# A top-k attention and two MLPs: first granules in halves, a second transposed tile, shared PSUM banks

## The chip, the cores and the metric

The kernel runs on one core of one Trainium2 chip. The metric is the device time of one execution in microseconds. The kernel before takes 1304.58 us, the median of 3 runs (1304.22 to 1305.43).

## What is computed

```
scores = q @ k.T / 8                      # 4 batches, 8 heads, 576 tokens, 64 wide
keep the 32 largest of each row, the rest to -1e9
attn = softmax(scores); o = attn @ v
x = o as 2304 tokens x 512
h = x @ w_in;  y = (h * sigmoid(1.702 h)) @ w_out            # layer 1: 512 -> 2048 -> 512
h = y @ w_in2; g = P(h) / (Q(h) + 1e-6); out = g @ w_out2    # layer 2, P and Q polynomials
```

q, k, v are float32 and the four weight matrices come as float64. Most products are made of float16 high and low parts, three matmuls in place of one; the last product of layer 2 is in float32.

## The kernel before, in words

**Tiles.** The 2304 tokens are 18 tiles of 128. A head of a tile is the unit of attention: 18 x 8 = 144 heads, done in this order. `attend` makes the scores (L584, into one of two PSUM tiles S of two banks), takes the top 32 with four MAX8 (L593) and three match-replace (L595) on VectorE, which write a copy W, then Prelu into E (L598, ScalarE), a bias on GpSimd (L599, L600), the exponential (L601), a float16 copy A and its low part (L603, L605), and a DMA transpose from A into AT (L609). W and E have two tiles each, A two, AT one. `attend_av` multiplies AT with V into the PSUM tile misc (L624), takes a reciprocal on VectorE (L634) and scales into x on ScalarE (L635).

**Granules.** When a tile's 8 heads are done, `x_done` splits x and transposes it by DMA into xh (L690). Granules are groups of tiles for the MLPs: eight of two tiles and two of one (GRAN). A layer of a granule runs in units: `u_h` multiplies into the PSUM tile h (L747), `u_act` evicts and computes the gate on ScalarE, VectorE and GpSimd (L768 to L808), `u_o` multiplies into acc0 and acc1, one bank for each tile of the granule (L829 for layer 2, L832 for layer 1). A unit of a pair of tiles takes 256 hidden columns, a unit of one tile 512. `y_done` (L847 and on) copies acc away, scales and transposes y for layer 2, `o_done` (L883) writes the result out.

**PSUM** has 8 banks: S takes four, acc0 and acc1 one each, h one and misc one. misc also serves the small sums over partitions in `total` (L308).

**Weights.** `w_load` brings in 32 blocks of float64 words, 1 MB each (L346), and three VectorE operations (L353, L355, L357) make float32 of them in one of three work slots. Layer 1's blocks are scaled and split into W1, which stays in SBUF. Layer 2's are written back to DRAM (L364, L385) and come in again through a ring of 7 slots by `u_load` (L720) for each granule. The ring's memory is also that of the two load slots and the three work slots, so its first 7 loads wait for every split.

**Order.** No queue is ordered at run time. A planner in the kernel takes each operation with an estimated duration and a due time counted in heads, adds an offset for its kind, engine and phase (OFF, PHASES), and picks on each engine, among those that can start earliest, the one that is due first; that is the instruction order written out. The u_h operations are chained in program order. The due time of layer 1 of a granule is 4.59 heads behind its last tile (LAV + MLAG). SPLIT lists the granules whose layer 1 runs as two halves of one tile, and LAGS says how many granules layer 2 runs behind:

```
seq, g2 = [], 0
for g in range(NG):
    seq += first_layer(g)
    while g2 < NG and g >= min(g2 + LAGS[g2], NG - 1):
        seq.append((2, g2, None))
        g2 += 1
```

With SPLIT = (0, 7, 8) and LAGS of 1 the order of layer 1 (a) and layer 2 (b) is a0 in two halves, a1, b0, a2, b1, a3, b2 and so on; a7 is in halves, and a9, b8, b9 come last. Since u_h is chained, b0 can't start ahead of a1.

## Time and profile before

| | |
|---|---|
| median of 3 runs | 1304.58 us (1304.22 to 1305.43) |
| span of the profiled execution, first to last instruction | 1298.1 us |
| its own device time | not listed; the span lies 6.5 us under the median |
| TensorE / VectorE / ScalarE / GpSimd busy | 1054.5 / 1038.0 / 1046.1 / 967.9 us |
| mean granted TensorE clock | 0.953 |

Times in the profile count from the first instruction. PE is TensorE, PEld its weight loads, DVE VectorE, ACT ScalarE, POOL GpSimd, SP the engine that issues the DMAs. A busy share is the time in which at least one instruction ran on the engine. The granted clock is TensorE's, as a share of full speed.

### The profile page before, as it was taken

What the parts mean: (1) busy time and instruction counts of PE and PEld (TensorE: products, weight loads), DVE (VectorE), ACT (ScalarE), POOL (GpSimd) and SP (SyncE); (2) the same over time, 40 slices, a digit from 0 to 9 for tenths busy, and PEclk for the clock granted to TensorE, in tenths of its full rate; (3) what the DMA queues carried; (4) which work ended last, traced back from release to release, by engine and by line L of the source; (5) the groups of instructions that cost most, each with busy time, mean ns of one, the idle gap of its engine ahead of it and who ended that gap; (6) DMA issues with size and microseconds to landing.
All of it is one profiled execution on the core that took longest, in us unless ns stands there. A gap on an engine that the chain in (4) does not pass through costs nothing.

```text
span 1298.1 us, 25266 instructions
## 1 busy us (share of the span) xinstructions
PE 1054.5 (81%) x8812; PEld 709.2 (55%) x8812; DVE 1038.0 (80%) x2227; ACT 1046.1 (81%) x1930; POOL 967.9 (75%) x1243
## 2 busy tenths in 40 slices
...
GB/s 237 203 186 175 150 263 255 228 252 175 145 73 158 195 170 106 144 231 168 141 216 211 85 171 218 147 115 181 182 106 154 205 117 83 209 99 154 115 247 183
DMA packets 366144, 222.40 MB, mean 171 GB/s; under 512 B 316608, under 2 KB 328896, under 8 KB 366016
## 3 DMA queue, kind: packets, MB, share of 16 engines
...
## 4 chain that ended last, share of the span: by engine, by line
PE 33%; DVE 22%; ACT 16%; POOL 15%; DMA 7%; issue 6%; SPq 1%; POOLq 0%; DVEq 0%; ACTq 0%
PE h L747 14%; PE acc L829 7%; DVE mx L593 7%; PE acc L832 6%; DVE W L595 6%; ACT t L768 6%; DMA AT<-A 6%; POOL t L772 5%; POOL A L605 3%; DVE ring L357 3%; PE misc L624 2%; PE S L584 2%; DVE ring L355 2%; POOL nm L599 2%; ACT E L601 2%
## 5 line engine op out<-in xcount | busy, mean ns | idle before, releaser
L772 POOL TENSOR_TENSOR t<-t,t 128x512 f32<-128x512 f32 x288 | 375.8, 1306 | 134.7 <-ACT t L768 67.4
L593 DVE MAX8 mx<-W 128x8 f32<-128x576 f32 x432 | 324.7, 755 | 6.4
L829 PE MATMUL acc<-ring,t 128*128 128x512 f32 x576 | 269.6, 600 | 12.0 <-POOL t L772 11.0
L747 PE MATMUL h<-xh,W 128*128 128x128 f16 (+1 forms) x2304 | 211.8, 251 | 7.7 <-ACT t L768 6.8
L605 POOL TENSOR_TENSOR A<-E,A 128x576 f16<-128x576 f32 x143 | 189.7, 1327 | 34.5 <-ACT A L603 29.6
L595 DVE MATCH_REPLACE8 W<-mx,W 128x576 f32<-128x576 f32 x288 | 213.5, 741 | 0.0
L747 PE MATMUL h<-yh,ring 128*128 128x256 f16 (+1 forms) x1920 | 203.5, 263 | 6.1 <-ACT t L768 5.3
L747 PEld LDWEIGHTS <-W 128*128 128x128 f16 x2304 | 183.8, 101 | 33.1 <-issue 15.7
L747 PEld LDWEIGHTS <-ring 128*128 128x128 f16 x1920 | 171.8, 98 | 47.1 <-issue 27.8
L584 PE MATMUL S<-K,qs 128*128 128x288 f16 (+1 forms) x640 | 120.7, 320 | 84.3 <-ACT E L598 67.3
L832 PE MATMUL acc<-W,gh 128*128 128x512 f16 x576 | 175.2, 386 | 0.9 <-ACT gh L806 0.9
L829 PEld LDWEIGHTS acc<-ring,t 128*128 128x128 f32 x576 | 101.1, 190 | 102.4 <-issue 85.0
L624 PE MATMUL misc<-V,AT 128*128 128x65 f16 (+5 forms) x2400 | 107.2, 203 | 56.5 <-DMA AT<-A 48.8
L601 ACT ACTIVATE E<-E,nm,ei 128x576 f32<-128x576 f32 x144 | 125.1, 869 | 33.2 <-POOL nm L600 31.4
L624 PEld LDWEIGHTS <-AT 128*128 128x128 f16 (+2 forms) x2400 | 97.3, 106 | 97.9 <-DMA AT<-A 76.4
L776 DVE SCALAR_TENSOR_TENSOR t<-t,ab,t 128x512 f32<-128x512 f32 x72 | 61.2, 850 | 108.8 <-ACT t L768 108.5
L598 ACT ACTIVATE E<-S,mx 128x576 f32<-128x576 f32 x144 | 106.5, 739 | 42.2 <-DVE mx L593 39.2
L584 PEld LDWEIGHTS <-qs 128*128 128x128 f16 (+1 forms) x640 | 65.6, 110 | 129.6 <-issue 88.6
L768 ACT ACTIVATE t<-h,cf 128x512 f32<-128x512 f32 (+1 forms) x160 | 93.7, 642 | 47.1 <-PE h L747 32.8
L593 DVE MAX8 mx<-S 128x8 f32<-128x576 f32 x144 | 108.8, 757 | 27.2 <-PE S L584 22.0
L599 POOL TENSOR_SCALAR nm<-mx,ei 128x1 f32<-128x1 f32 x144 | 82.2, 571 | 44.9 <-DVE mx L593 35.7
L832 PE MATMUL acc<-W,gl 128*128 128x512 f16 x288 | 110.9, 385 | 5.4 <-POOL gl L808 5.3
...
## 6 DMA issues: line engine op xcount, KB each, us to landing
ring<-scr SPq DMA_DIRECT2D x160, 512.0 KB, 4.0
...
scr<-ring SPq DMA_DIRECT2D x8, 512.0 KB, 7.5
```

Of the source, the lines that this page charges most:

```text
L584: PE.matmul(s[:n, c, :SH], qs[:, 2 * (h % 4) + x, :n], K[:, h % 2, c * SH:(c + 1) * SH], start=(x == 0), stop=(x == 1))
L593: op("DVE", dve(S, not r), lambda r=r: DVE.max(mx[:, r], w.t if r else sv()), [w if r else s], [mx], prio)
L595: op("DVE", dve(S, not r) + 0.068, lambda r=r: DVE.match_replace(w.t if r else two(w.t), mx[:, r], w.t if r else sv(), NEG), [mx, w if r e ...
L599: op("POOL", 2 * PTINY, lambda: (POOL.tensor_scalar(nm.t, mx[:, 0, 0:1], mx[:, 3, 7:8], es(), ALU.subtract, ALU.mult), POOL.tensor_scalar( ...
L601: op("ACT", act(S) + 2 * APA, lambda: ACT.activation(e.t, e.t, AF.Exp, bias=nm.t, scale=es()), [e, nm, ei], [e], prio)
L605: lo = lambda en: en.tensor_tensor(A[:, 1, :S], e.t, A[:, 0, :S], ALU.subtract)
L624: PE.matmul(ps[r0:r0 + n, :hi - lo], at[:kp, x, j, r0:r0 + n], V[:kp, h % 2, j, lo:hi], start=(j == 0 and lo == D and x == 0), stop=(j == ...
L747: PE.matmul(o, w[:, half, kd * 256 + jj * P: kd * 256 + (jj + 1) * P], xy[:, tl, l * ND + kd, :], start=(n == 0), stop=(n == 3 * ND - 1))
L768: op("ACT", act(w, True) + APA, lambda f2=f2, c=c: ACT.activation(dst[:, c], src[:, c], func, bias=bias(f2) if bias else 0.0, scale=sc(f2) ...
L772: op("POOL", pool_tt(512), lambda: POOL.tensor_tensor(o.t, x.t, y.t, f), [x, y], [o], prio, alt=("DVE", dve(512), lambda: DVE.tensor_tenso ...
L829: PE.matmul(acc[j].t, u.gate[:, c], w[:, jj * DM:(jj + 1) * DM], start=st, stop=sp)
L832: PE.matmul(acc[j].t, l[:, c], w[:, half, jj * DM:(jj + 1) * DM], start=(st and n == 0), stop=(sp and n == 2))
```

## The change

What it does:

- **SPLIT** goes from (0, 7, 8) to (0, 1, 2, 7, 8), and **LAGS** begins with 0.5, 0.5. A layer 2 may now stand behind half a granule. The order becomes a0 in halves, first half of a1, b0, second half of a1, first half of a2, b1, second half of a2, a3, b2, a4 and so on as before.
- **Staged splits** (STAGE = 8): the first 8 of layer 1's 16 blocks are made float32 in the room of W1 that blocks 8 to 15 fill later, and only the later ones in the work slots. The first write to such room (the Square, L370) waits for the block staged there.
- **AT** has two tiles (NAT = 2).
- **W and E** become one buffer with three tiles (NE = 3).
- **h and misc** share two banks with the tag hm, and acc0 and acc1 become two banks of one tag acc. The planner hands these banks out in the order of use.
- **y_copy**: the copies of acc leave `y_done` and run for each tile as soon as its part of layer 1 ends. xh gets two fixed tiles.
- **The planner**: several estimated durations, the phases and nearly all offsets are new (some 250 offsets in place of 69), so the order on each engine changes. W2P, the due time of layer 2's weight blocks, goes from 4.62 to 3.4.

No instruction of the computation is added or removed, but for the shapes of halves in layer 1 of granules 1 and 2.

```diff
-            cv = slot("work", work)
+            n_w = 2 * f2 + j
+            over = []
+            if layer == 1:
+                region = lambda i: W1t[:, i // 2, 2 * (i % 2):2 * (i % 2) + 2].rearrange("p a n -> p (a n)")
+                if n_w < STAGE:
+                    cv = staged[2 * NPAIR - STAGE + n_w] = token(f"stage{n_w}")
+                    cv.t = region(2 * NPAIR - STAGE + n_w)
+                if n_w in staged:
+                    over = [staged.pop(n_w)] if n_w >= STAGE else []
+            if layer == 2 or n_w >= STAGE:
+                cv = slot("work", work)
...
             op("ACT", act(CW) + 0.2, lambda hl=hl, val=val, wi=wi: ACT.activation(
-                hl().rearrange("p a n -> p (a n)").bitcast(F32), val(), AF.Square, accum_out=wsq[:, f2, wi:wi + 1]), [cv], [dst, sqb], prio)
+                hl().rearrange("p a n -> p (a n)").bitcast(F32), val(), AF.Square, accum_out=wsq[:, f2, wi:wi + 1]), [cv], [dst, sqb] + over, prio)
...
     def misc():
-        return buf("misc", [P, 512], F32, NMISC, pp)
+        return buf("hm" if HM else "misc", [P, 512], F32, HM or NMISC, pp)
...
-        w = buf("W", [P, S], F32, 2)
-        e = buf("E", [P, S], F32, NE)
+        w = e = buf("W", [P, S], F32, NE)
...
-        u.ph = buf("h", [P, 512], F32, NH, pp)
+        u.ph = buf("hm" if HM else "h", [P, 512], F32, HM or NH, pp)
...
-                ACC[u.layer, u.g, j] = buf(f"acc{j}", [P, 512], F32, NACC, pp)
+                ACC[u.layer, u.g, j] = buf("acc", [P, 512], F32, NACC, pp)
...
+    def y_copy(g, tiles, prio):
+        for j in tiles:
+            aj = ACC.pop((1, g, j))
+            yc = YC[g, j] = buf("yc", [P, DM], F32, NYC)
+            op("ACT", act(512, True), lambda yc=yc, aj=aj: ACT.activation(yc.t, aj.t, AF.Copy), [aj], [yc], prio - 1e-3,
+               alt=("DVE", dve(512, True), lambda yc=yc, aj=aj: DVE.tensor_copy(yc.t, aj.t)))
...
-        seq += first_layer(g)
-        while g2 < NG and g >= min(g2 + LAGS[g2], NG - 1):
-            seq.append((2, g2, None))
-            g2 += 1
+        for n, part in enumerate(first_layer(g)):
+            seq.append(part)
+            while g2 < NG and g + (n + 1) / len(first_layer(g)) >= min(g2 + 1 + LAGS[g2], NG):
+                seq.append((2, g2, None))
+                g2 += 1
...
-NACC = 1
+NACC = 2
-NE = 2
+NE = 3
-NAT = 1
+NAT = 2
+NMISC = 1
+HM = 2
-SPLIT = (0, 7, 8)
-LAGS = (1, 1, 1, 1, 1, 1, 1, 1, 1, 1, 1, 1, 1, 1, 1, 1, 1, 1)
+SPLIT = (0, 1, 2, 7, 8)
+LAGS = (0.5, 0.5, 1, 1, 1, 1, 1, 1, 1, 1, 1, 1, 1, 1, 1, 1, 1, 1, 1, 1)
-W2P = 4.62
+W2P = 3.4
+STAGE = 8
...
-    ('attend', 'PE'): 0.16,
-    ('attend', 'PE', 0): 0.86,
+    ('attend', 'PE'): -11.3,
+    ('attend', 'PE', 0): 1.59,
+    ('attend', 'PE', 1): 4.16,
+    ('attend', 'PE', 2): 6.98,
+    ('attend', 'PE', 3): 4.46,
-    ('attend_av', 'PE', 0): 1.95,
+    ('attend_av', 'PE'): -5.57,
...
-PHASES = (16.0, 48.0, 130.0)
-FREE = ("t", "misc")
+PHASES = (1, 41.34, 154.07)
+FREE = ("t", "misc", "acc", "hm")
```

## Rows read from the trace of the kernel before

**Rows 1.** The page: busy totals of the engines.

```profile
PE 1054.5 (81%) x8812; PEld 709.2 (55%) x8812; DVE 1038.0 (80%) x2227; ACT 1046.1 (81%) x1930; POOL 967.9 (75%) x1243
```

**Rows 2.** By stretch: length; PE, PEld, DVE, ACT, POOL busy; clock; DMA share; GB/s.

```profile
0.00:300.00 300.00, 119.99 (x1034) 83.14 (x1035) 275.83 (x582) 205.94 (x370) 209.65 (x267) 0.88 0.83 218
300.00:345.00 45.00, 24.39 (x195) 15.43 (x193) 43.38 (x120) 32.45 (x76) 29.36 (x67) 0.54 0.79 152
345.00:600.00 255.00, 240.52 (x1996) 162.11 (x1996) 222.52 (x488) 228.11 (x425) 204.91 (x282) 0.99 0.69 154
600.00:1105.00 505.00, 487.95 (x4182) 330.38 (x4180) 466.28 (x988) 453.19 (x831) 412.43 (x533) 1.00 0.71 156
1105.00:1298.00 193.00, 181.68 (x1411) 118.18 (x1409) 29.98 (x54) 126.42 (x233) 111.53 (x98) 1.00 0.52 167
```

**Rows 3.** The same for instructions on ring alone (on DVE, the weight splits).

```profile
0.00:300.00 300.00, 0.00 (x0) 0.00 (x0) 117.76 (x96) 81.88 (x96) 54.35 (x24) 0.88 0.83 218
```

**Rows 4.** The same for mx alone: DVE, ACT, POOL; last the whole span.

```profile
0.00:300.00 300.00, 147.59 (x286) 20.55 (x28) 26.79 (x28) 0.88 0.83 218
300.00:345.00 45.00, 39.46 (x75) 5.09 (x7) 2.90 (x7) 0.54 0.79 152
...
sum 1298.00, DVE 774.03 ACT 106.45 POOL 82.17; mean DVE 258.01 ACT 35.48 POOL 27.39
```

**Rows 5.** Timeline of SP's queue: last split store, transposes of tiles 2, 3, 4, 5, 7.

```profile
276.19 0.34 SPq L385 DMA_DIRECT2D scr<-yh  x1
...
296.71 1.25 SPq L690 DMA_TRANSPOSE xh<-xs  x1
...
340.72 1.39 SPq L690 DMA_TRANSPOSE xh<-xs  x1
...
406.51 1.34 SPq L690 DMA_TRANSPOSE xh<-xs  x1
...
455.88 1.23 SPq L690 DMA_TRANSPOSE xh<-xs  x1
...
563.03 1.23 SPq L690 DMA_TRANSPOSE xh<-xs  x1
```

**Rows 6.** Timeline of PE: the first h of a layer of a granule.

```profile
345.02 2.74 PE L747 MATMUL h<-xh,W 128*128 128x256 f16 x12
...
401.79 1.47 PE L747 MATMUL h<-yh,ring 128*128 128x256 f16 x12
...
469.89 1.47 PE L747 MATMUL h<-xh,W 128*128 128x256 f16 x12
...
520.76 1.47 PE L747 MATMUL h<-yh,ring 128*128 128x256 f16 x12
...
580.51 2.78 PE L747 MATMUL h<-xh,W 128*128 128x256 f16 x24 [0.16 <-ACT t L768]
```

**Rows 7.** VectorE's waits, 345 to 600 us: us in total, times, longest.

```profile
DVE r L634 <- PE misc L624: 12.2, 9, 3.3
```

**Rows 8.** Timeline of VectorE: the first weight split.

```profile
14.45 1.34 DVE L353 TENSOR_SCALAR ring<-ring 128x1024 int32<-128x1024 int32 x1 [2.14 <-DMA ring<-in_moe_w_in_dram]
```

**Rows 9.** TensorE's waits, 345 to 1105 us.

```profile
PE misc L624 <- DMA AT<-A: 16.5, 18, 2.2
...
PE h L747 <- ACT t L768: 4.9, 7, 1.7
```

**Rows 10.** Timelines of VectorE and GpSimd: a head's first match-replace, its low part, a later head.

```profile
502.29 0.75 DVE L595 MATCH_REPLACE8 W<-mx,S 128x576 f32<-128x576 f32 x1
...
510.72 1.28 POOL L605 TENSOR_TENSOR A<-E,A 128x576 f16<-128x576 f32 x1 [0.31 <-ACT A L603]
...
521.91 0.75 DVE L595 MATCH_REPLACE8 W<-mx,S 128x576 f32<-128x576 f32 x1
```

**Rows 11.** The chain that ended last, in order of time: start, us, instructions.

```profile
508.60 2.62 PE h L747 x24
...
1074.36 2.68 PE h L747 x48
```

More of the change, by code (lines that the diff above doesn't have):

```diff
@@ L191, in schedule @@
             if o.eng == "SP":
[L192 to L193 removed]
+                dma = max(dma, t + 1.4) + o.bytes / 270e3
+                end = dma + 1.0
             o.finish = end
@@ L325 @@
     work = [flat(ring[:, j:j + 1]) for j in range(4, NR)]
+    xhtiles = [cp.tile([P, 2, 2 * ND, P], F16, name=f"xh{j}") for j in range(2)]
+    xhslot = []
+    staged = {}
     parts = [ring[:, j] for j in range(NR)]
@@ L946 @@
             p = max(p, W2P + NPAIR * WR + 0.1)
+        if layer == 1:
+            at(p + OLAG, y_copy, g, u.tiles, p)
         if done:
@@ new lines @@
+    ('attend', 'PE', 2): 6.98,
+    ('attend', 'PE', 3): 4.46,
+    ('attend', 'POOL'): -1.25,
+    ('attend', 'POOL', 0): 30.62,
+    ('attend', 'POOL', 1): 0.16,
+    ('attend', 'POOL', 2): -0.07,
+    ('attend', 'POOL', 3): 1.2,
+    ('attend', 'SP', 0): 15.48,
+    ('attend', 'SP', 1): 2.28,
+    ('attend', 'SP', 3): 5.96,
+    ('attend_av', 'ACT'): -9.25,
+    ('attend_av', 'ACT', 0): -4.32,
+    ('attend_av', 'ACT', 1): 4.8,
+    ('attend_av', 'ACT', 2): -4.54,
+    ('attend_av', 'ACT', 3): 4.01,
@@ new lines @@
+    ('attend_av', 'DVE'): -0.38,
+    ('attend_av', 'DVE', 0): -0.47,
+    ('attend_av', 'DVE', 1): 0.53,
+    ('attend_av', 'DVE', 2): 0.04,
+    ('attend_av', 'DVE', 3): -5.99,
+    ('attend_av', 'PE'): -5.57,
+    ('attend_av', 'PE', 1): -1.87,
+    ('attend_av', 'PE', 2): -0.49,
+    ('attend_av', 'PE', 3): 3.23,
+    ('k_prep', 'ACT'): -0.47,
+    ('k_prep', 'ACT', 0): -17.74,
+    ('k_prep', 'ACT', 1): -0.07,
+    ('k_prep', 'ACT', 2): -1.3,
+    ('k_prep', 'ACT', 3): 0.24,
+    ('k_prep', 'DVE'): -1.39,
@@ new lines @@
+    ('k_prep', 'SP', 2): 0.38,
+    ('k_prep', 'SP', 3): 5.25,
+    ('o_done', 'ACT'): -2.76,
+    ('o_done', 'ACT', 0): 5.21,
+    ('o_done', 'ACT', 1): -3.85,
+    ('o_done', 'ACT', 2): 3.72,
+    ('o_done', 'ACT', 3): -0.82,
+    ('o_done', 'DVE', 0): -0.25,
+    ('o_done', 'DVE', 1): -2.02,
+    ('o_done', 'DVE', 2): -0.23,
+    ('o_done', 'DVE', 3): -6.73,
+    ('o_done', 'SP'): 1.56,
+    ('o_done', 'SP', 1): 0.32,
+    ('o_done', 'SP', 3): -0.51,
+    ('q_prep', 'ACT'): 5.63,
+    ('q_prep', 'ACT', 0): 2.4,
@@ new lines @@
+    ('u_act', 'DVE', 0): 2.87,
+    ('u_act', 'DVE', 1): -4.86,
+    ('u_act', 'DVE', 2): -7.24,
+    ('u_act', 'DVE', 3): 0.24,
+    ('u_act', 'POOL'): 0.17,
+    ('u_act', 'POOL', 0): 0.84,
+    ('u_act', 'POOL', 1): -7.77,
+    ('u_act', 'POOL', 2): -0.16,
+    ('u_act', 'POOL', 3): 3.54,
+    ('u_h', 'PE'): 0.27,
+    ('u_h', 'PE', 0): 0.94,
+    ('u_h', 'PE', 1): 2.67,
+    ('u_h', 'PE', 2): -0.35,
+    ('u_h', 'PE', 3): 0.02,
+    ('u_load', 'SP'): 33.63,
+    ('u_load', 'SP', 0): 4.41,
+    ('u_load', 'SP', 1): -4.38,
@@ new lines @@
+    ('u_load', 'SP', 2): -10.14,
+    ('u_load', 'SP', 3): -3.0,
+    ('u_o', 'PE'): 0.26,
+    ('u_o', 'PE', 0): 1.76,
+    ('u_o', 'PE', 1): 14.87,
+    ('u_o', 'PE', 2): -0.47,
+    ('v_prep', 'ACT'): -1.23,
+    ('v_prep', 'ACT', 0): -2.32,
+    ('v_prep', 'ACT', 1): 1.49,
+    ('v_prep', 'ACT', 3): 3.83,
+    ('v_prep', 'DVE'): -2.66,
+    ('v_prep', 'DVE', 0): -10.23,
+    ('v_prep', 'DVE', 1): 0.29,
+    ('v_prep', 'DVE', 2): -10.09,
+    ('v_prep', 'DVE', 3): -1.89,
+    ('v_prep', 'POOL'): -0.61,
@@ new lines @@
+    ('v_stat', 'PE'): -2.34,
+    ('v_stat', 'PE', 0): 0.79,
+    ('v_stat', 'PE', 1): 13.58,
+    ('v_stat', 'PE', 3): 3.54,
+    ('v_stat', 'POOL'): -1.35,
+    ('v_stat', 'POOL', 0): 3.66,
+    ('v_stat', 'POOL', 2): -1.07,
+    ('v_stat', 'POOL', 3): 2.9,
+    ('v_stat', 'SP', 1): -8.34,
+    ('v_stat', 'SP', 2): -8.88,
+    ('v_stat', 'SP', 3): 9.64,
+    ('w_consts', 'DVE'): 10.05,
+    ('w_consts', 'DVE', 1): -1.21,
+    ('w_consts', 'DVE', 2): 14.72,
+    ('w_load', 'ACT'): -3.82,
+    ('w_load', 'ACT', 1): 3.0,
@@ new lines @@
+    ('w_load', 'ACT', 2): 26.43,
+    ('w_load', 'ACT', 3): -5.86,
+    ('w_load', 'DVE'): -0.96,
+    ('w_load', 'DVE', 1): 0.22,
+    ('w_load', 'DVE', 2): 0.38,
+    ('w_load', 'DVE', 3): 0.17,
+    ('w_load', 'PE'): -4.95,
+    ('w_load', 'PE', 0): 5.39,
+    ('w_load', 'PE', 2): -0.76,
+    ('w_load', 'POOL'): -2.33,
+    ('w_load', 'POOL', 1): 3.28,
+    ('w_load', 'POOL', 2): 0.06,
+    ('w_load', 'POOL', 3): 1.07,
+    ('w_load', 'SP'): 4.28,
+    ('w_load', 'SP', 0): -6.34,
+    ('w_load', 'SP', 1): -3.53,
```

218 lines of the change are left out of this document (138 added, 80 removed).

## The prediction

> **What bounds the kernel now.** I read the page first, then a table by stretch, then lines, timelines and waits of single stretches. The page's totals say little: TensorE, VectorE and ScalarE are each busy for four fifths of the span [rows 1]. The table by stretch shows why: there are two regimes [rows 2]. Up to 345 us VectorE is full (0 to 300: 275.8 us; 300 to 345: 43.4 of 45) and TensorE is not (120.0 of 300; 24.4 of 45), at a granted clock of 0.88 and then 0.54, where 1.00 is 2.4 GHz and 0.50 is 1.2 GHz. From 345 on TensorE is busy 240.5 + 488.0 + 181.7 = 910 of 953 us at clock 0.99 to 1.00. Whatever lets TensorE enter that second regime earlier, with work that does not run out again, moves the end almost one for one.
>
> What holds it back until 345? VectorE's first 300 us hold the 96 split operations of 32 weight blocks, 117.8 us [rows 3], and 147.6 us of top-k. All top-k work is 774.0 us [rows 4], 5.37 us for each of 144 heads, so 27.5 heads are done at 300 us and 34.8 at 345. The transposes of x tell when a tile is ready for layer 1: tile 2 at 296.7 us, tile 3 at 340.7, tile 7 at 563.0; the last split weights go to DRAM at 276.2 [rows 5]. TensorE's timeline shows layer 1 of granule 1 starting at 345.0, as soon as tile 3 has landed, though tile 2 has lain there for 44 us; then layer 2 of granule 0 from 401.8, layer 1 of granule 2 from 469.9, layer 2 of granule 1 from 520.8, layer 1 of granule 3 from 580.5 [rows 6]. Between 300 and 345 TensorE has nothing but heads.
>
> **Part by part.** *Granules 1 and 2 in halves, layer 2 half a granule behind* (SPLIT, LAGS). The order becomes: layer 1 of tile 2, layer 2 of granule 0, tile 3, tile 4, layer 2 of granule 1, tile 5, granule 3, and from there as before. Layer 1 of tile 2 can start when its transpose has landed, 296.7 + some 4 = 300.5 us, and not at 345.0: **-44.5 us**. Is there work enough behind it? Prices from [rows 6]: layer 1 of a tile (401.8 - 345.0) / 2 = 28.4 us, of a tile of granule 2 (520.8 - 469.9) / 2 = 25.5, layer 2 of granules 0 and 1 68.1 and 59.7, all with the heads between. Tile 2 until 329, layer 2 of granule 0 until 397, tile 3 (ready at 345) until 425, tile 4 (transposed at 406.5 [rows 5]) until 451, layer 2 of granule 1 until 511, tile 5 (455.9) until 536. None of these has to wait. Then granule 3 needs tile 7, which the old trace has ready at 563.0 + 4 = 567: that is what is late next. Layer 2's loads from DRAM come earlier too. Between 600 and 1105 us they run beside the heads at a DMA share of 0.71, and TensorE is 97% busy [rows 2], so I cost them at nothing; without that cover a late load holds up the whole of TensorE's queue.
>
> *The wait for tile 7.* Lower bound: at VectorE's pace of 300 to 345 us, 39.5 us of top-k in 45 us [rows 4] or 6.1 us a head, the 32 heads behind tile 3 take 196 us, and tile 7 lands at 541. TensorE arrives at 536, plus 3 us for heads that it ran before 345 in the old order, so 1 to 2 us are lost. Upper bound: the pace stays and 27 us are lost. VectorE has the room: 32.5 of its 255 us between 345 and 600 were idle [rows 2], and what it waited for there most was TensorE itself, 12.2 us for attention products [rows 7]. The new table of offsets brings just these forward on TensorE (attend from +0.16 to -11.3, attend_av from 0 to -5.57). I take **+5**, near the lower end.
>
> *Heads that TensorE still owes.* At 300.5 us 27.5 heads are done, not 34.8. Between 300 and 345 TensorE did nothing but 7.3 heads and a few sums, 24.4 us at clock 0.54 [rows 2], which is at most 24.4 x 0.54 = 13 us at full clock. At least it is nothing, where a head fits into a gap that is idle now. I take **+9**, nearer the row, since the sums go off.
>
> *Staged splits.* The first 8 of 16 layer-1 blocks use room of W1 that is filled later, not the 3 work slots. VectorE's work is the same. It idled 300.0 - 275.8 = 24.2 us before 300 [rows 2], but 14.45 us pass before the first split has data [rows 8]. So some 10 us can be had at most. The added wait: the Square of a later block stands behind the stage that lies in its room, with the heads' exponentials behind it on ScalarE and VectorE waiting for these; it delays the same operations, so I bound the loss by the same 10 us. I take **-3**. Layer-2 blocks start 1.2 heads earlier (W2P); they end 20 us ahead of tile 2's transpose, and that hides it.
>
> *Second AT tile.* A head's transpose need not wait until the last product has read its tile. Between 345 and 1105 us TensorE waited for that DMA for 16.5 us [rows 9]. Between 0 and -16.5 I take **-6**: a wait that ends sooner still has the transfer's own time. SP issues as many transposes as before, and fewer loads are queued behind a waiting one.
>
> *h and products on two common banks, acc on two common banks, y_copy by tile.* Eviction of h held TensorE for 4.9 us there [rows 9]; the gain is that at most, 0 to -5, the loss is rival D: **-2**. y_copy is the same 18 copies ahead of the rest of y_done, on a ScalarE that has 10% free (below): 0, and 0.6 us each if it were full.
>
> *One tile for W and E, three of them.* A head holds it from its first match-replace, 502.29, to the end of the low part, 510.72 + 1.28 = 512.0: 9.7 us. The third head behind it starts at 521.9 [rows 10]. 10 us of slack cover it: 0.
>
> *Halves.* Layer 1 of a 128-token tile takes units of 48 matmuls in 2.68 us, of a pair 24 in 2.62 [rows 11]. Four halves of 4 units, 16 x 0.06 = **+1**.
>
> *The order on every engine* is planned anew. No row prices that. TensorE's 43 us of idle time from 345 on are all that a better order could return there, and a worse one could lose as much. I take 0 and keep 15 us either way.
>
> Sum: -44.5 + 5 + 9 - 3 - 6 - 2 + 1 = -40.5. The profiled span is 1298.1 us, 6.5 under the median of 1304.6; only the span is shown for that execution, so I take the 6.5 around it as unchanged: 1304.6 - 40.5 = **1264 us**.
>
> **Row against rule.** The rows make TensorE the bound: from 345 to 1105 us it is busy (240.5 + 488.0) / 760 = 96%, ScalarE (228.1 + 453.2) / 760 = 90% [rows 2]. Matmuls of 256 columns follow each other every 109 ns there (24 in 2.62 us [rows 11]) at clock 1.00. The Trainium skill (Perfetto Trace Analysis, section Identifying the Most-Contended Engine) holds matmul busy time for no good measure, and would have weight-load time and FLOPs read instead. By that rule, with weight loads at 492 of these 760 us, ScalarE would be the engine to look at, and the sum would be that of rival B. I go by the rows.
>
> **Rivals.**
> (B) *ScalarE is the bound.* Then early MLP work can use only what ScalarE had free between 300 and 345, 45.0 - 32.5 = 12.5 us [rows 2]: 1304.6 - 12.5 = 1292. The wait for tile 7 at its upper bound gives nearly the same, -40.5 + 22 = -18.5, 1286. For it: 90% busy. Against: TensorE's waits for ScalarE's h are 4.9 us in 760 [rows 9].
> (C) *All bounds on the good side:* -44.5 + 1 + 0 - 10 - 16.5 - 5 + 1 = -74, 1231.
> (D) *Slower: the shared banks.* A product that holds a bank until its reciprocal and scaling are done keeps the next h out, with all of TensorE queued behind it. Price: 0.7 us (4.9 us in 7 waits for h's eviction [rows 9]) up to the 1.7 of the longest; there are 144 units. At 0.7 us the gain is gone from 58 such waits on; with one in each unit it is 1264 + 101 = 1365. Against: two banks for two kinds hold no less than one for each.
> (E) *The change doesn't do what it says:* layer 2's loads wait for the last split, and if the new order ends the splits later than 345 us, layer 2 is not early: 1304.
>
> **Numbers.** A measurement tells 0.2% (2.6 us) from no change; the three runs lie within 1.2 us. Forecast 0.56 (its own range 1249 to 1279, 15 us for the order), B 0.17, C 0.14, D 0.10, E 0.03. Faster by over 0.2%: forecast, C and nearly all of B, 0.85; within 0.2%: E and the edge of B, 0.05; slower: D, 0.10. The range takes in the forecast, B and most of C: 1235 to 1300.
>
> **What would show it.** Layer 1 of tile 2 starts near 300 us and layer 2 of granule 0 near 330; the clock is near 1.00 from 305 on; granule 3's layer 1 starts near 541; TensorE is 95% busy from 300 on. It is wrong if tile 2's transpose itself moves far from 297, if TensorE has a gap over 10 us before granule 3, if waits of h or of products for a bank pass 40 us, or if VectorE waits for W.

## The result and the profile after

The changed kernel takes **1271.4 us** (median of 4 runs, 1269.5 to 1273.3) against 1304.4 of the kernel before in the same comparison: a ratio of **0.9756 [0.9737, 0.9775]**, 33.0 us less. The profiled execution has a span of 1267.8 us and took 1269.74 us, so 1.9 us lie around the span. By the span it is 1298.1 - 1267.8 = 30.3 us less. One run of e9 below took 1488.2 us at a granted clock of 0.75 and is left out of its median.

The page of the changed kernel, its head and the busy totals of the engines ([rows 1] before):

```profile
span 1267.8 us, 26108 instructions
...
PE 1048.1 (83%) x9196; PEld 717.8 (57%) x9196; DVE 1017.3 (80%) x2220; ACT 1045.7 (82%) x1970; POOL 969.5 (76%) x1242
```

The totals again say little. The table by stretch of the changed kernel (length; PE, PEld, DVE, ACT, POOL busy; clock; DMA share; GB/s) answers to [rows 2]; its last two lines cut 345 to 570 us more finely:

```profile
0.00:300.00 300.00, 119.86 (x1062) 86.29 (x1063) 272.50 (x573) 205.55 (x379) 211.30 (x264) 0.91 0.77 208
300.00:345.00 45.00, 41.49 (x431) 31.49 (x431) 41.83 (x107) 41.11 (x84) 39.18 (x69) 0.92 0.90 195
345.00:600.00 255.00, 234.13 (x2267) 160.70 (x2265) 242.00 (x548) 236.76 (x473) 210.55 (x307) 0.97 0.75 167
600.00:1105.00 505.00, 495.84 (x4203) 337.07 (x4201) 439.01 (x957) 454.87 (x837) 419.01 (x531) 1.00 0.73 163
...
345.00:545.00 200.00, 192.93 (x1881) 130.35 (x1879) 189.18 (x412) 188.76 (x379) 166.66 (x224) 1.00 0.79 179
545.00:570.00 25.00, 14.09 (x138) 10.85 (x137) 24.59 (x72) 18.67 (x37) 16.29 (x41) 0.66 0.68 129
```

Between 300 and 345 us TensorE is now busy 41.5 us instead of 24.4: the second regime begins some 50 us earlier. But from 545 to 570 there is a hole: TensorE 14.1 of 25 us at a granted clock of 0.66, while VectorE is full, 24.6 of 25.

The hole in TensorE's timeline, and the layers' starts that answer to [rows 6]:

```profile
293.92 3.55 PE L761 MATMUL hm<-xh,W 128*128 128x128 f16 x36
...
326.52 3.65 PE L761 MATMUL hm<-yh,ring 128*128 128x256 f16 x32
...
544.98 0.38 PE L846 MATMUL acc<-W,gl 128*128 128x512 f16 x1
545.19 0.62 PE L638 MATMUL hm<-V,AT 128*128 128x65 f16 x15
...
552.96 1.00 PE L638 MATMUL hm<-V,AT 128*128 128x65 f16 x15 [0.60 <-DMA AT<-A]
...
560.29 1.00 PE L638 MATMUL hm<-V,AT 128*128 128x65 f16 x15 [2.68 <-DMA AT<-A]
...
565.46 1.99 PE L761 MATMUL hm<-xh,W 128*128 128x256 f16 x12
```

The last layer-1 product of tile 5 ends at 545.4, and granule 3's layer 1 starts at 565.5. In between TensorE has only heads, some five of them, and a few sums, and waits for most. What granule 3 lacks is tile 7, as SP's queue shows (last split store, then the transposes of tiles 2 to 7; [rows 5] before):

```profile
285.30 0.34 SPq L400 DMA_DIRECT2D scr<-yh  x1
...
290.67 1.27 SPq L704 DMA_TRANSPOSE xh<-xs  x1
...
358.77 2.78 SPq L704 DMA_TRANSPOSE xh<-xs  x1
...
424.61 1.75 SPq L704 DMA_TRANSPOSE xh<-xs  x1
...
478.14 1.23 SPq L704 DMA_TRANSPOSE xh<-xs  x1
...
510.97 1.24 SPq L704 DMA_TRANSPOSE xh<-xs  x1
...
561.23 1.42 SPq L704 DMA_TRANSPOSE xh<-xs  x1
```

Tile 2 comes 6.0 us earlier than before, tile 3 18.1 us later, tile 7 only 1.8 us earlier (561.2 against 563.0).

Tile 7's heads were there earlier than that. The scaling of its last head into x (ScalarE), the first transpose of granule 2's y (SP) and the split of tile 7's x (ScalarE), then before, the last head and the split:

```profile
549.80 0.29 ACT L649 ACTIVATE x<-hm,r 128x64 f32<-128x64 f32 x1
...
554.95 1.23 SPq L883 DMA_TRANSPOSE yh<-xs  x1
...
558.99 0.61 ACT L701 ACTIVATE xs<-x 128x512 f16<-128x512 f32 x1
```

```profile
559.71 0.32 ACT L635 ACTIVATE x<-misc,r 128x64 f32<-128x64 f32 x1
560.05 0.63 ACT L687 ACTIVATE xs<-x 128x512 f16<-128x512 f32 x1
```

The last head is done at 550.1 us, 9.9 us earlier than before. But the split, which before followed at once, comes 8.9 us behind it. It writes into xs, the buffer in which the float16 halves of x and of y wait for their transposes. xs has two tiles, and its tag is not among those that are handed out in the order of use. Granule 2's y holds both, and its scale is known only behind the last layer-1 product of tile 5. The view of xs from 540 to 565 us gives the time from the issue of a y transpose to its landing:

```profile
DMA to landing us min/median/max: 3.2/3.2/3.4
```

So the first xs tile is free at 558.2 us. In e7 (below) the same split stands in the timeline with its wait named:

```profile
576.55 0.63 ACT L702 ACTIVATE xs<-x 128x512 f16<-128x512 f32 x1 [0.15 <-DMA yh<-xs]
```

The end of the hole is thus a chain that starts where the hole starts: last layer-1 product, granule 2's y, its transpose, tile 7's split, its transpose, granule 3. Before, the y of granule 2 was transposed from 549.2 us on, ahead of tile 7's last head, and nothing waited.

**Where the 30.3 us come from**, by marks of the two timelines: layer 1 of tile 2 starts at 293.9 and not 345.0, **-51.1**. From there to the end of TensorE's work on tile 5 it takes 545.4 - 293.9 = 251.5 us, where before 580.5 - 345.0 = 235.5 lay between the first h of granule 1 and the first of granule 3, **+16.0**. The hole is 565.5 - 545.4 = **+20.1**. From granule 3's start to the end it takes 702.3 us, before 717.6, **-15.3**. Sum -30.3.

TensorE's waits of the changed kernel that answer to [rows 9] (us in total, times, longest), first from 345 to 600 us, then from 600 to 1105:

```profile
PE hm L638 <- DMA AT<-A: 7.1, 7, 2.7
...
PE hm L761 <- ACT t L782: 2.0, 1, 2.0
...
PE hm L638 <- DMA AT<-A: 3.3, 5, 1.5
...
PE hm L761 <- ACT x L649: 0.5, 1, 0.5
```

### The profile page after: what moved, and what is told of

It is laid out like the page before. It is cut to its first block, busy times and chain, and to the rows that moved or that the text cites. A ratio compares the mean times of both kernels' runs of the same rounds, so it can differ in the third digit from the quotient of the medians.

```text
span 1267.8 us, 26108 instructions
## 1 busy us (share of the span) xinstructions
PE 1048.1 (83%) x9196; PEld 717.8 (57%) x9196; DVE 1017.3 (80%) x2220; ACT 1045.7 (82%) x1970; POOL 969.5 (76%) x1242
## 4 chain that ended last, share of the span: by engine, by line
PE 35%; DVE 26%; ACT 14%; POOL 13%; issue 7%; DMA 5%; SPq 0%; POOLq 0%; DVEq 0%; ACTq 0%
PE hm L761 14%; DVE mx L607 9%; PE acc L843 9%; DVE W L609 8%; PE acc L846 8%; POOL t L786 4%; ACT t L782 4%; DMA AT<-A 3%; POOL A L619 3%; PE S L599 2%; PE hm L638 2%; DVE ring L370 2%; POOL nm L613 2%; ACT W L615 1%; POOL gl L822 1%
## 5 line engine op out<-in xcount | busy, mean ns | idle before, releaser
L761 PE MATMUL hm<-xh,W 128*128 128x128 f16 (+1 forms) x2688 | 218.8, 241 | 4.2 <-ACT t L782 2.9
L761 PEld LDWEIGHTS <-W 128*128 128x128 f16 x2688 | 195.5, 102 | 28.7 <-issue 11.2
L619 POOL TENSOR_TENSOR A<-W,A 128x576 f16<-128x576 f32 x144 | 192.1, 1335 | 24.0 <-ACT A L617 21.0
L761 PE MATMUL hm<-yh,ring 128*128 128x256 f16 (+1 forms) x1920 | 203.0, 262 | 1.0 <-ACT x L649 0.9
L599 PE MATMUL S<-K,qs 128*128 128x288 f16 (+1 forms) x640 | 114.2, 308 | 72.1 <-ACT W L612 50.9
L790 DVE SCALAR_TENSOR_TENSOR t<-t,ab,t 128x512 f32<-128x512 f32 x72 | 67.7, 941 | 115.7 <-ACT t L782 115.5
L615 ACT ACTIVATE W<-W,nm,ei 128x576 f32<-128x576 f32 x144 | 125.8, 873 | 27.6 <-POOL nm L614 26.4
L638 PE MATMUL hm<-V,AT 128*128 128x65 f16 (+5 forms) x2400 | 104.0, 200 | 50.8 <-DMA AT<-A 40.0
L612 ACT ACTIVATE W<-S,mx 128x576 f32<-128x576 f32 x144 | 106.9, 743 | 26.0 <-DVE mx L607 21.6
L782 ACT ACTIVATE t<-hm,cf 128x512 f32<-128x512 f32 (+1 forms) x160 | 94.5, 645 | 33.0 <-PE hm L761 32.9
L613 POOL TENSOR_SCALAR nm<-mx,ei 128x1 f32<-128x1 f32 x144 | 87.9, 610 | 34.8 <-DVE mx L607 16.2
```

Of the source, the lines that this page charges most:

```text
L599: PE.matmul(s[:n, c, :SH], qs[:, 2 * (h % 4) + x, :n], K[:, h % 2, c * SH:(c + 1) * SH], start=(x == 0), stop=(x == 1))
L613: op("POOL", 0.75, lambda: (POOL.tensor_scalar(nm.t, mx[:, 0, 0:1], mx[:, 3, 7:8], es(), ALU.subtract, ALU.mult), POOL.tensor_scalar(nm.t, ...
L615: op("ACT", act(S) + 2 * APA, lambda: ACT.activation(e.t, e.t, AF.Exp, bias=nm.t, scale=es()), [e, nm, ei], [e], prio)
L619: lo = lambda en: en.tensor_tensor(A[:, 1, :S], e.t, A[:, 0, :S], ALU.subtract)
L638: PE.matmul(ps[r0:r0 + n, :hi - lo], at[:kp, x, j, r0:r0 + n], V[:kp, h % 2, j, lo:hi], start=(j == 0 and lo == D and x == 0), stop=(j == ...
L761: PE.matmul(o, w[:, half, kd * 256 + jj * P: kd * 256 + (jj + 1) * P], xy[:, tl, l * ND + kd, :], start=(n == 0), stop=(n == 3 * ND - 1))
```

## The experiments

In the expectations, theory T is the prediction's own mechanism, that the halves and the early layer 2 let TensorE's full regime begin earlier; rival O is that the gain is that of the new order and the other parts; rival G is that the heads' pace sets the time and the hole before the next granule only moves. Where a text uses another letter, it says there what that stands for. Four marks tell the runs apart (us of the profiled execution): the start of layer 1 of tile 2, or of granule 1 where that is whole, the transpose of tile 7, the start of granule 3's layer 1, and the rest from there to the end of the span. Runs e1 to e4, e5 to e8 and e9 to e12 each shared a chip and their runs of the kernel before (medians 1301.6, 1301.8 and 1304.0); the ratios are to these. e1, e2 and e4 to e8 are planned anew, so each has an order of its own; e3, e9, e10 and e11 keep the changed kernel's.

| run | median us | ratio | layer 1 starts | tile 7 | granule 3 | rest |
|---|---|---|---|---|---|---|
| before | 1304.4 | | 345.0 | 563.0 | 580.5 | 717.6 |
| after | 1271.4 | 0.9756 [0.9737, 0.9775] | 293.9 | 561.2 | 565.5 | 702.3 |
| e1_before_half | 1304.2 | 1.0013 [0.9991, 1.0035] | 299.9 | 578.1 | 581.2 | 722.9 |
| e2_after_whole | 1291.6 | 0.9906 [0.9874, 0.9937] | 346.7 | 553.9 | 581.8 | 710.2 |
| e3_after_top24 | 1266.4 | 0.9711 [0.9683, 0.9740] | 293.0 | 557.2 | 561.4 | 704.1 |
| e4_after_half3 | 1285.6 | 0.9861 [0.9830, 0.9893] | 293.6 | 572.8 | | |
| e5_old_plan | 1313.8 | 1.0096 [1.0071, 1.0121] | 314.1 | 588.8 | 592.0 | 721.9 |
| e6_nat1 | 1315.1 | 1.0116 [1.0094, 1.0138] | 307.0 | 592.4 | 595.6 | 712.9 |
| e7_plan_top24 | 1292.7 | 0.9933 [0.9916, 0.9951] | 293.3 | 579.5 | 582.7 | 708.6 |
| e8_plan_lessact | 1277.7 | 0.9817 [0.9802, 0.9832] | 293.4 | 565.8 | 569.5 | 704.6 |
| e9_pe_early | 1265.9 | 0.9740 [0.9695, 0.9785] | 295.0 | 562.2 | 566.5 | 702.6 |
| e10_pe_late | 1261.3 | 0.9695 [0.9659, 0.9731] | 294.6 | 562.7 | 566.9 | 695.4 |
| e11_act_all | 1266.4 | 0.9731 [0.9697, 0.9765] | 292.6 | 558.1 | 562.3 | 703.5 |
| e12_control | 1269.8 | 0.9752 [0.9711, 0.9793] | 293.7 | 561.0 | 565.2 | 705.4 |

### One part with and without the other: e1 and e2

**e1_before_half** is the kernel before with the halves, the earlier layer 2 and the per-tile y_copy that these need, and nothing else:

```diff
+    def y_copy(g, tiles, prio):
+        for j in tiles:
+            aj = ACC.pop((1, g, j))
...
-        seq += first_layer(g)
-        while g2 < NG and g >= min(g2 + LAGS[g2], NG - 1):
-            seq.append((2, g2, None))
-            g2 += 1
+        for n, part in enumerate(first_layer(g)):
+            seq.append(part)
+            while g2 < NG and g + (n + 1) / len(first_layer(g)) >= min(g2 + 1 + LAGS[g2], NG):
+                seq.append((2, g2, None))
+                g2 += 1
...
-SPLIT = (0, 7, 8)
-LAGS = (1, 1, 1, 1, 1, 1, 1, 1, 1, 1, 1, 1, 1, 1, 1, 1, 1, 1)
+SPLIT = (0, 1, 2, 7, 8)
+LAGS = (0.5, 0.5, 1, 1, 1, 1, 1, 1, 1, 1, 1, 1, 1, 1, 1, 1, 1, 1)
```

> The kernel before with SPLIT (0, 1, 2, 7, 8), LAGS 0.5, 0.5 and the copies of acc by tile alone; offsets, banks, AT, W and E and the splits as before. Theory T (TensorE's full stretch starts with layer 1 of tile 2, and is held up once by tile 7): layer 1 of tile 2 near 300 us, a gap before granule 3 of 10 to 25 us, 1272 to 1284 us. Rival O (the gain is the new order, banks, staging and second AT tile): 1298 to 1306 us.

No gain at all: 1.0013 [0.9991, 1.0035], the time of O. Yet the start came as T has it. In e1's timelines of SP (tile 7) and PE (the end of tile 5's work, the first h of granule 3), and its table by stretch:

```profile
578.12 1.23 SPq L690 DMA_TRANSPOSE xh<-xs  x1
```

```profile
546.09 0.38 PE L832 MATMUL acc<-W,gl 128*128 128x512 f16 x1
...
581.23 2.72 PE L747 MATMUL h<-xh,W 128*128 128x256 f16 x12 [1.03 <-DMA xh<-xs]
```

```profile
300.00:345.00 45.00, 40.05 (x456) 30.13 (x456) 37.87 (x90) 42.69 (x95) 38.13 (x65) 0.98 0.72 152
345.00:545.00 200.00, 189.93 (x1835) 127.93 (x1834) 177.00 (x379) 180.94 (x362) 160.22 (x217) 1.00 0.78 169
545.00:570.00 25.00, 9.57 (x76) 6.14 (x75) 24.97 (x67) 15.51 (x29) 13.08 (x31) 0.62 0.52 100
```

TensorE is 40.1 of 45 us busy from 300 to 345 and finishes its MLP work at 546.5, all as in the changed kernel. But tile 7 slips from 563.0 to 578.1, and a hole of 581.2 - 546.5 = 34.8 us eats everything. Here it is the heads: tile 7's last one is in x at 576.1, and its split follows at once. VectorE, which sets the heads' pace where TensorE is free (24.97 of 25 us in the hole), was idle for 7.1 us from 300 to 345 and 23.0 us from 345 to 545. As I read it, what the early MLP work gains TensorE, it takes from the heads, which TensorE and ScalarE have to serve as well. So in this order the early start alone is worth nothing; it needs heads that keep up.

**e2_after_whole** is the changed kernel with granules 1 and 2 whole again and layer 2 a whole granule behind:

```diff
-SPLIT = (0, 1, 2, 7, 8)
-LAGS = (0.5, 0.5, 1, 1, 1, 1, 1, 1, 1, 1, 1, 1, 1, 1, 1, 1, 1, 1, 1, 1)
+SPLIT = (0, 7, 8)
+LAGS = (1, 1, 1, 1, 1, 1, 1, 1, 1, 1, 1, 1, 1, 1, 1, 1, 1, 1, 1, 1)
```

> The changed kernel with SPLIT (0, 7, 8) and LAGS of 1 as before, all other parts kept. Theory T: layer 1 of granule 1 waits for tile 3, which landed later here (358.8 us was its issue), so 1293 to 1312 us. Rival O: the other parts carry the gain, at most 1280 us.

0.9906, some 10 us faster and just under T's range. Granule 1 starts at 346.7, when tile 3 (transposed at 342.96) has landed: without halves the other parts don't start the regime earlier. Tile 7 comes at 553.9, 9 us earlier than before, but TensorE is not ready for it until 581.8. The gain stands in the rest, 710.2 us instead of 717.6. So halves alone 0, the rest alone -10, both -33: more than the sum. That each takes away the bound that hides the other's gain is my reading; both runs are planned anew with numbers that were fitted to another kernel, and what that costs them is not known.

### Another order, and one part less: e4 to e8

**e4_after_half3** also halves granule 3 and brings its layer 2 forward, so that TensorE could start tile 6 without waiting for tile 7:

```diff
-SPLIT = (0, 1, 2, 7, 8)
-LAGS = (0.5, 0.5, 1, 1, 1, 1, 1, 1, 1, 1, 1, 1, 1, 1, 1, 1, 1, 1, 1, 1)
+SPLIT = (0, 1, 2, 3, 7, 8)
+LAGS = (0.5, 0.5, 0.5, 1, 1, 1, 1, 1, 1, 1, 1, 1, 1, 1, 1, 1, 1, 1, 1, 1)
```

> The changed kernel with granule 3 in halves as well and layer 2 of granule 2 between them (LAGS 0.5, 0.5, 0.5). Theory T: tile 6 (transposed at 511) fills the gap, tile 7 is there when its turn comes, 1250 to 1258 us. Rival G (the gap only moves, since the heads slow down while layer 2 uses ScalarE and GpSimd): a gap of 10 us or more before granule 4, 1264 to 1273 us.

Slower than the changed kernel, 0.9861 against 0.9756, and outside the ranges of both theories. The hole moves to granule 4. In e4's timelines, the transpose of tile 9 (SP), the last product ahead of granule 4 and its first h (PE), then the table by stretch:

```profile
683.26 1.38 SPq L704 DMA_TRANSPOSE xh<-xs  x1
```

```profile
662.19 0.38 PE L846 MATMUL acc<-W,gl 128*128 128x512 f16 x1
...
686.55 2.74 PE L761 MATMUL hm<-xh,W 128*128 128x256 f16 x12 [0.23 <-DMA xh<-xs]
```

```profile
645.00:690.00 45.00, 29.91 (x290) 20.10 (x287) 43.85 (x113) 40.14 (x97) 29.83 (x58) 0.75 0.76 160
```

TensorE runs out of MLP work at 662.6 and waits until 686.5, with VectorE full (43.9 of 45). The hole only moves, as rival G has it: MLP work moved ahead of what feeds it is paid for at the next granule. But the heads are not all of it: tile 9's last one is in x at 671.0 and its split starts at 680.7, behind the first transpose of granule 3's y (676.4). The new hole is 23.9 us where the old one was 20.1, and granule 4 starts 13.2 us later than in the changed kernel (686.5 against 673.3), so some 9 us more went into the work ahead of it; no run says why.

**e5_old_plan** keeps the changed kernel's structure, but gives the planner its old durations, offsets, phases and the old W2P and SWITCH:

```diff
-    TINY, PTINY, APD, APA = 0.119, 0.29, 0.12, 0.1
+    TINY, PTINY, APD, APA = 0.075, 0.28, 0.061, 0.1
...
-PHASES = (1, 41.34, 154.07)
+PHASES = (16.0, 48.0, 130.0)
...
-W2P = 3.4
+W2P = 4.62
```

> The changed kernel with all its structure (halves, staging, two AT tiles, shared banks, one W/E) but the planner's old numbers: durations, offsets, phases, W2P and SWITCH of before. Theory R (the new order keeps the heads fed while layer 2 is early): tile 7 comes after 570 us, 1292 to 1305 us. Rival P (the freed buffers and banks do it, under either order): 1268 to 1282 us.

1.0096: all of the gain is gone, and 12 us more, beyond the range of either theory. Layer 1 of tile 2 starts at 314.1 us, tile 7 comes at 588.8. (SWITCH, another number of the planner, goes from 0.83 to 1.36 with the change.) **e6_nat1** takes the second AT tile away and leaves the rest, with the new offsets:

```diff
-NAT = 2
+NAT = 1
```

> The changed kernel with one AT tile. Theory P: TensorE's waits for AT come back (16.5 us between 345 and 1105 before, now some 10) and heads fall behind, 1277 to 1290 us. Theory R: the second tile is worth little, under 1276 us.

1.0116, tile 7 at 592.4, again beyond both ranges. From 300 to 545 us TensorE is busy 216.8 us in e6, where the changed kernel has 41.5 + 192.9 = 234.4. Neither run is the price of one part: the planner makes a new order each time, with a table of offsets that was fitted to another kernel. What they show is that structure and table go together: either without the other loses 40 us and more. That this is misfit, and not the worth of the part, is argued.

**e7_plan_top24** leaves out one of the four top-k rounds of heads 24 to 63 and lets the planner know it; **e8_plan_lessact** leaves out ScalarE operations of the early MLP work, planned anew:

```diff
-        for r in range(4):
+        kk = 2 if 24 <= i < 64 else 3
+        for r in range(kk + 1):
```

> As the run that left out one round of the top-k in heads 24 to 63, but the planner knows it and orders anew: 60 us less on VectorE. Theory V (VectorE paces the heads up to tile 7): tile 7 transposed before 545 us, gap under 10 us, 1250 to 1260 us. Theory S (ScalarE, 94% busy between 300 and 500, paces them together with TensorE): tile 7 within 8 us of 561, 1262 to 1272 us.

```diff
-                op("ACT", act(512) + APA, lambda: ACT.activation(e.t, e.t, AF.Identity, bias=ones[:, 0:1]), [e], [e], prio)
+                if u.g not in (1, 2):
+                    op("ACT", act(512) + APA, lambda: ACT.activation(e.t, e.t, AF.Identity, bias=ones[:, 0:1]), [e], [e], prio)
...
-            op("ACT", act(512) + APA, lambda: ACT.activation(z.t, z.t, AF.Ln, bias=c1), [z], [z], prio, table="ln")
-            op("ACT", act(512), lambda: ACT.activation(z.t, z.t, AF.Exp, scale=-1.0), [z], [z], prio)
+            if u.g >= 2:
+                op("ACT", act(512) + APA, lambda: ACT.activation(z.t, z.t, AF.Ln, bias=c1), [z], [z], prio, table="ln")
+                op("ACT", act(512), lambda: ACT.activation(z.t, z.t, AF.Exp, scale=-1.0), [z], [z], prio)
```

> The changed kernel without the tanh's plus one in layer 1 of granules 1 and 2 and without Ln and Exp in layer 2 of granules 0 and 1, planned anew: some 34 us less on ScalarE between 294 and 545 us, nothing less on VectorE. Theory S: tile 7 transposed before 550 us, 1250 to 1260 us. Theory V: tile 7 stays within 8 us of 561, 1264 to 1272 us.

Both are slower than the changed kernel though they do less: 1292.7 and 1277.7, above every range, tile 7 at 579.5 and 565.8. A planned kernel with an operation taken out doesn't tell the price of the operation, since the order is lost with it. **e12_control** asks how much a new order costs by itself: one weight of the planner is nudged, and some 1750 instructions stand elsewhere.

```diff
-UW = 0.998
+UW = 1.002
```

> The changed kernel with one planner number moved by 0.4% (UW 0.998 to 1.002), planned anew; the same instructions in another order. Theory N (a new order alone moves the time by as much as single parts did): 5 us or more from 1271, up or down, and tile 7 moves with it. Rival: within 3 us.

0.9752 [0.9711, 0.9793] against 0.9756: nothing. But the two orders part only at 901 us; ahead of that every engine's instructions come in the changed kernel's order, as far as the profile lists them. TensorE's timelines where they part, of the changed kernel and of e12:

```profile
900.68 3.91 PE L843 MATMUL acc<-ring,t 128*128 128x512 f32 x8
```

```profile
900.11 1.88 PE L843 MATMUL acc<-ring,t 128*128 128x512 f32 x4
```

So e12 shows that a new order of the last 370 us need not cost anything, and its marks up to granule 3 are those of a repeat. Of the stretch in which e5 to e8 lose it says nothing. For that, e7 and e3 (below) are the better pair: they leave out the same work and differ in order alone, and e7 takes 0.9933 where e3 takes 0.9711, some 26 us more. An order by itself can cost that much; that e5, e6 and e8 lose in the same way is argued, not shown. The next runs therefore keep the changed kernel's order instruction for instruction and only leave work out.

### The same order with less work: e3, e9, e11, e10

**e3_after_top24** has e7's omission in the changed kernel's own order (the operations are planned, and nothing is issued for them), **e9_pe_early** leaves out the gl products of layer 1 of granules 1 and 2 on TensorE, **e11_act_all** operations of ScalarE in granules 0 to 6:

```diff
+        kk = 2 if 24 <= i < 64 else 3
...
-            op("DVE", dve(S, not r), lambda r=r: DVE.max(mx[:, r], w.t if r else sv()), [w if r else s], [mx], prio)
+            op("DVE", dve(S, not r), lambda r=r: None if r > kk else DVE.max(mx[:, r], w.t if r else sv()), [w if r else s], [mx], prio)
...
```

> The changed kernel, same order; heads 24 to 63 (tiles 3 to 7) leave out one MAX8 and one match-replace of the top-k and take the 24th value as the threshold, 1.5 us of VectorE for each of 40 heads. Theory V (VectorE paces the heads that tile 7 waits for): tile 7 is transposed 15 us or more before 561, the gap of 20 us before granule 3 closes, 1250 to 1257 us. Rival B (ScalarE paces them): tile 7 moves under 5 us, 1267 to 1273 us.

```diff
-                    for n, (l, half) in enumerate(((u.gh, 0), (u.gh, 1), (u.gl, 0))):
...
+                    ops = ((u.gh, 0), (u.gh, 1), (u.gl, 0))[:2 if u.g in (1, 2) else 3]
+                    for n, (l, half) in enumerate(ops):
```

> The changed kernel, same order; the products of the low half gl are left out in layer 1 of granules 1 and 2, 64 matmuls of 0.216 us, 13.8 us of TensorE between 294 and 545 us. Theory Q (TensorE's full queue, in its planned order, holds the heads back up to tile 7): tile 7 transposed 8 us or more before 561, 1256 to 1263 us. Rival S (ScalarE or VectorE holds them): tile 7 within 3 us of 561, 1267 to 1272 us.

```diff
-                op("ACT", act(512) + APA, lambda: ACT.activation(e.t, e.t, AF.Identity, bias=ones[:, 0:1]), [e], [e], prio)
+                op("ACT", act(512) + APA, lambda: None if u.g in (1, 2, 4, 5, 6) else ACT.activation(e.t, e.t, AF.Identity, bias=ones[:, 0:1]), [e], [e], prio)
...
-            op("ACT", act(512) + APA, lambda: ACT.activation(z.t, z.t, AF.Ln, bias=c1), [z], [z], prio, table="ln")
+            op("ACT", act(512) + APA, lambda: None if u.g in (0, 1, 3, 4, 5) else ACT.activation(z.t, z.t, AF.Ln, bias=c1), [z], [z], prio, table="ln")
...
```

> The changed kernel, same order; the tanh's plus one is left out in layer 1 of granules 1, 2, 4, 5, 6 and Ln and Exp in layer 2 of granules 0, 1, 3, 4, 5, some 84 us less on ScalarE. Theory T: 1262 to 1272 us, tile 7 within 5 us. Rival B: under 1250 us.

The table by stretch, 345 to 545 us, of e3, e9 and e11 (the changed kernel's own line stands above):

```profile
345.00:545.00 200.00, 193.85 (x1904) 131.32 (x1902) 156.61 (x330) 189.81 (x381) 166.94 (x226) 0.99 0.80 180
```

```profile
345.00:545.00 200.00, 186.43 (x1837) 127.03 (x1835) 189.68 (x411) 189.52 (x378) 166.58 (x223) 0.99 0.81 179
```

```profile
345.00:545.00 200.00, 193.14 (x1901) 131.12 (x1900) 190.57 (x417) 168.72 (x337) 165.10 (x226) 0.99 0.81 179
```

In e3 VectorE's busy time falls from 189.2 to 156.6 us, and TensorE's stays at 194: tile 7 comes 4.0 us earlier. VectorE's waits of e3 in the stretch say for what it now waits, TensorE's products and scores (in the changed kernel 1.4 and 2.4 us):

```profile
DVE r L649 <- PE hm L639: 15.4, 17, 2.0
DVE mx L608 <- PE S L599: 15.3, 16, 2.7
```

In e9 TensorE's falls from 192.9 to 186.4, and VectorE's stays at 190: tile 7 comes 1.0 us later, MLP work ends at 545.1 as in the changed kernel, and TensorE idles. In e11 ScalarE's falls from 188.8 to 168.7, and tile 7 comes 3.2 us earlier. Part of these shifts is there from the start: the transpose of tile 2, ahead of nearly all that is left out, goes at 290.7 us in the changed kernel and at 289.7, 291.6 and 289.2 in e3, e9 and e11. Counted from it tile 7 comes 3.1, 0 and 1.7 us earlier. That is far from the 15 us of V in e3 and the 8 us of Q in e9, and ScalarE's relief brings no more. (The profiled run of e9 is its slowest, 1271.1 us; two others took 1265.8 and 1265.9, so the early products may be worth some 4 us against e12.) So from 300 to 545 us **three engines are nearly full at once**, TensorE at (41.5 + 192.9) / 245 = 96%, VectorE and ScalarE, (41.1 + 188.8) / 245, at 94%, and what one of them is spared comes back as its own idle time, in e3 as waits for TensorE. No run spares two at once.

Nor does the hole change: from the last product of tile 5 to granule 3 it is 20.1 us in the changed kernel, and 20.0, 21.3 and 20.3 in e3, e9 and e11 (541.4 to 561.4, 545.1 to 566.5, 542.0 to 562.3), 20.0 in e10 and e12. The chain by way of xs explains that, and the heads don't: tile 7's last head is in x at 546.3, 550.3 and 546.9 us in e3, e9 and e11, and its split starts 8.6, 9.7 and 8.9 us later, 13.5 to 14.9 us behind tile 5's last product as in the changed kernel (13.6).

**e10_pe_late** leaves out the same gl products, but of granules 4, 5 and 6, where TensorE has no hole (the lines around it are e9's):

```diff
+                    ops = ((u.gh, 0), (u.gh, 1), (u.gl, 0))[:2 if u.g in (4, 5, 6) else 3]
```

> The changed kernel, same order; the products of gl are left out in layer 1 of granules 4, 5 and 6, 96 matmuls, 20.7 us of TensorE behind 673 us. Theory T (TensorE is the bound of the second regime): 1249 to 1256 us. Rival B (ScalarE is): 1264 to 1272 us.

The pages' busy totals of e10 and of e11, which takes its work away from ScalarE:

```profile
PE 1031.1 (82%) x9100; PEld 707.8 (56%) x9100; DVE 1016.3 (81%) x2220; ACT 1046.2 (83%) x1970; POOL 969.2 (77%) x1242
```

```profile
PE 1043.6 (82%) x9196; PEld 713.7 (56%) x9196; DVE 1021.6 (81%) x2220; ACT 985.4 (78%) x1850; POOL 970.1 (77%) x1242
```

In e10 TensorE has 1048.1 - 1031.1 = 17.0 us less to do, and from granule 3 to the end it takes 695.4 us instead of 702.3, -6.9. By the medians it is 8.5 us faster than e12, which ran on the same chip, and all four runs of e10 lie below all four of e12; by the ranges this is neither T (1249 to 1256) nor B. In e11 ScalarE has 60.3 us less to do, over the whole kernel, and that end stretch takes 703.5 us, against 702.3 in the changed kernel and 705.4 in e12; the median is 3.3 us below e12's, as T has it. So behind granule 3 TensorE is the nearest bound and ScalarE is not, but it is not the only one. From 673 to 1060 us, the table by stretch of the changed kernel and of e10:

```profile
673.00:1060.00 387.00, 381.37 (x3375) 261.78 (x3374) 359.34 (x793) 351.17 (x647) 319.96 (x419) 1.00 0.71 156
```

```profile
673.00:1060.00 387.00, 370.04 (x3323) 256.00 (x3324) 359.92 (x798) 356.00 (x656) 326.34 (x424) 1.00 0.72 158
```

TensorE's idle time grows from 5.6 to 17.0 us of 387. Its waits of e10 in this stretch name for what most of all, ScalarE's Prelu, which frees the score banks (0.5 us in the changed kernel):

```profile
PE S L599 <- ACT W L612: 6.9, 10, 1.3
```

## Why the prediction was right, and where it was wrong

The time came out 7 us above the forecast of 1264, in its own range and with its sign. The mechanism was right, TensorE's second regime starts half a granule earlier. One term, the wait for tile 7, was mis-sized by 15 us: the heads came later than summed, and a buffer behind them was left out. By spans the terms were off by -3.6 (start), +6.0 (work behind it), +15.1 (wait) and -7.3 us (rest); that half of this cancels is luck. By two of its own signs, a gap over 10 us ahead of granule 3 and VectorE waiting for W, the prediction is wrong in those steps.

- **The start.** Taken as -44.5, with -3 for the splits; measured -51.1. Tile 2 came 6.0 us earlier than I had left it. The staged splits didn't do that: the last split store went out at 285.3, 9.1 us *later* than in [rows 5], and VectorE's busy time up to 300 us fell only from 275.8 to 272.5. What got shorter is the way from top-k to x. By the Prelu instructions that read mx, one for each head, 27 heads had begun theirs when tile 2 (24 heads) was transposed before, and 25 after. e6, with one AT tile, has tile 2 at 300.2; that fits, but its order is another one, so the cause is argued, not shown.
- **The work behind it.** I had layer 2 of granule 0 from 329, tile 3 from 397, layer 2 of granule 1 from 451, the end of tile 5 at 536. It was 326.5, 387.5, 453.4 and 545.4. The terms for owed heads and halves, +10, were +16.0.
- **The wait for tile 7: the step that failed.** It was taken as +5 and measured 20.1, inside its bounds of 1 and 27 but near the upper one. The lower bound had tile 7 transposed at 537; the trace has it at 561.2, 24 us later. *Some 16 us are the heads.* Tile 7's last head is in x at 550.1, and before, 3.0 us lay between that and the transpose (560.0 to 563.0), so by its heads alone it would have gone at some 553. My 537 had 192 / 6.1 = 31.5 heads behind 345 us. At 345 only 33 heads had passed by the Prelus and not 34.8, since the new order has fewer top-k instructions ahead of 300 us (274, before 286 [rows 4]), and 66 had begun theirs at 553: 33 heads, 9 us more, and each took 208 / 33 = 6.3 us, 7 us more. *Some 8 us are a wait that the sum did not have:* the split of tile 7's x stands behind granule 2's y in the two tiles of xs, as shown above. The prediction counted the heads that tile 7 needs, and no buffer behind them.
- **VectorE's room.** I counted on its 32.5 idle us for a faster pace. In the changed kernel it used most of them (242.0 of 255 us busy, before 222.5); before, 32 heads took the 218 us from 345 to 563, 6.8 us each. As I read it, that paid for what e1 lost; tile 7's last head came 9.9 us earlier than before, and xs gave 8 of them back. Why the pace did not rise further is argued, not shown: TensorE, for which VectorE waited [rows 7], now had MLP work in just that time.
- **The second AT tile**, -6: TensorE's waits for that transfer fell from 16.5 to 7.1 + 3.3 = 10.4 us. That is the size forecast, though much of the 7.1 lies in the hole, where nothing is gained, and no run shows what the tile is worth in time. **Shared banks**, -2: the waits of h for ScalarE fell from 4.9 to 2.7 us, but the products and sums now wait for ScalarE's reads of the same banks, 5.0 us in 345 to 1105 us where they had no such wait. So the waits show no gain. Rival D is far off all the same, which wanted over 40 us. **W and E in one tile**, 0: VectorE waited for it four times, 8.4 us in all, so the 10 us of slack did not always cover it.
- **The rest behind granule 3** was to give the 8 us of these terms, and gave 15.3. TensorE is busy 495.8 of 505 us there, before 488.0. The order was taken as 0 with 15 either way. e2 has 7.4 us of it without halves; the remainder is not divided further, and e12, with the same order up to 901 us, has 3 us less of it.
- **Around the span** I put 6.5 us, the median of before less its span. In every execution that shows both it is 1.7 to 2.4 us, so the profiled execution of before was a quick one, and the comparison of spans (-30.3) understates that of medians (-33.0).
- **Rival B and the rule.** ScalarE as the bound gave 1286 to 1292. e11 took 60.3 us from ScalarE and won 2 to 5 us (span, median), e10 17.0 from TensorE and won 6 to 10. By the rule of the Trainium skill (Perfetto Trace Analysis, section Identifying the Most-Contended Engine), matmul busy time would have been set aside; here the rows on it named the nearer bound. What I overstated is that TensorE would give back "almost one for one": e10 gave back about half. **Rival E** fell with layer 2 of granule 0 at 326.5.
- **What stays open:** whether a third tile of xs, or another turn for it, closes the hole; no run has one. Had the split followed the last head as it did before, tile 7's transpose would have gone at some 553 us and granule 3 some 4 us later, a hole of 12 us: an estimate from the rows above. In the fixed order no engine's relief closed it, and with e7's relief and a new plan it stayed at 20 us (562.5 to 582.7) and moved later. No kernel with the whole computation was faster than the changed one beyond its interval.
